# Three rounded passes for the inverse DFT-64 of seven batches, with new places for constants and weight loads

## The chip, the cores and the metric

The kernel runs on one core of a Trainium2 chip. The metric is the time of one execution on the device in microseconds (us), the median of several runs; less is better.

## What is computed

A Fourier mixing layer is followed by a gated feed-forward layer. Input x has 8 batches of 3008 rows and 256 columns; the model is 256 wide, the feed-forward layer 2048.

```python
X = np.fft.rfft(x, axis=1)
Xr, Xi = (X.real.astype(np.float32), X.imag.astype(np.float32))
Yr = Xr @ w_r - Xi @ w_i + b_r
Yi = Xr @ w_i + Xi @ w_r + b_i
Yr = np.sign(Yr) * np.maximum(np.abs(Yr) - lam, 0.0)   # lam = 0.01, Yi alike
y = np.fft.irfft(Yr + 1j * Yi, n=x.shape[1], axis=1)
h = y.reshape(B * S, D) @ w_in
g = h * (1.0 / (1.0 + np.exp(-1.702 * h)))
return (g @ w_out).astype(np.float32)
```

## The kernel before

**The Fourier part.** 3008 is 64 x 47, so the transform is done as a DFT of 47 and one of 64. For each batch, `spectral` lists the work in two halves. The first has 16 steps: `load_x` brings a piece of x, `stage_a` multiplies it by the DFT-47 constants on TensorE, ScalarE copies the result out (aev) and it is stored to a DRAM scratch. The second has 12 steps (sp), each for two frequencies of the DFT-47: `load_b` reads br back with its constants kr, `stage_b` does the forward DFT-64, `stage_mix` the product with w_r and w_i, the bias and the soft threshold (into mv), `move` carries mv by four DMAs into yr with real and imaginary rows stacked, and `stage_inv` does the inverse DFT-64 of yr, copies it out (iev) and stores it. `tokens` then reads it as ur, does the inverse DFT-47 and writes the columns of y that the feed-forward part reads. Stages lag each other: inverse step n - 5 stands beside forward step n.

**The feed-forward part.** It goes over 24 tiles of rows, and for each over 8 pieces q of the 2048 columns. From tile 2 on (PLAIN = 2) a product of 2x2 blocks is done with 7 products in place of 8. Weights arrive as float64 and are turned into pairs of rounded float32 numbers (`fetch`, `turn`, `combine`); `keep` writes the results to DRAM, from where `load_up` (wq), `Group.load` (wd) and `load_wo` (wo) fetch them again.

**Two ways to multiply.** A plain float32 matmul is one instruction in the program and two records in the trace. The other way splits both operands into a rounded part and a rest (`split`: ScalarE casts, VectorE subtracts) and does three passes in the float32r type (`mm3`, lines 147 to 149). The inverse DFT-64 is plain float32 in every batch (line 434), and its constants kv differ from step to step, so each `move` also loads 128 KB of kv into one of two buffers (KV = 2).

**Order and buffers.** A list scheduler sets the order of each engine when the kernel is built; at run time every engine and every DMA queue takes its work in that order. The Fourier steps of batches 1 and 2 fill tiles 0 and 1; those of later batches are spread over the tiles before they are due. The tag w2 is a pool of 7 buffers that xr, aev, br, mv, mt, yr, iev and ur share; the tag g has 13 for raw weights, x pieces and gelu results; wd has 3. SP issues nearly all DMAs; POOL issues the aev stores of batches 1 to 7, the raw weight loads of the main loop and the writes of `keep`.

Of the kernel before, what the change touches and what calls it, by code (L numbers as in the profile page):

```python
# [21 lines left out]
LAM = 0.01  # L22
# [5 lines left out]
TILE = 2 * TOK  # L28
NQ = DFF // 256
NP = 7  # L30
W2 = 7
PLAIN = 2
EARLY = 3
TK, JIT, RAW, WQ, WD, PT, KV, CO, ZT = 7, 3, 13, 3, 3, 5, 2, 1, 1
TINY = float(np.uint32(896 << 20).view(np.float32))


# [15 lines left out]
def constants():  # L53
    def ang(a, b, n):
        return 2.0 * np.pi * ((np.outer(a, b)) % n) / n

    n1, n2, k1, k2 = np.arange(N1), np.arange(N2), np.arange(N1), np.arange(NS)
    t47 = ang(n2, k2, N2)
    t64 = ang(n1, k1, N1)


    fa = np.zeros((48, NS, 2))
    fa[:N2, :, 0] = np.cos(t47)
    fa[:N2, :, 1] = -np.sin(t47)
# [24 lines left out]
    binv0 = inv * np.concatenate([w0r, w0i])[:, None]  # L89
    binv0[:, N1:] = 0.0  # L90


    ai = np.zeros((NS, 2, 2, 2, N2))
    for p in range(2):
        ai[:, 0, p, p] = np.cos(t47.T)
        ai[:, 1, p, p] = -np.sin(t47.T)
    ai = ai.reshape(96, 94)

    signs = np.ones((NS, 2 * N1, 1))
    signs[:, N1:, 0] = sign.T  # L100
    v = signs * binv
    v[0] = binv0
    v = v.reshape(NS // 2, 2, 2 * N1, 2 * N1).transpose(0, 2, 1, 3)
    kbs = np.stack([b, v], axis=1)

    pack = np.zeros((128, 190), np.float32)
    pack[:96, 0:96] = a
    pack[:96, 96:190] = ai
    return pack, kbs.astype(np.float32)


@with_exitstack
def fourier_mix_then_gated_ffn(ctx: ExitStack, tc: tile.TileContext, x, w_r, w_i, b_r, b_i, w_in, w_out, pack, kbs, out):
# [38 lines left out]
    kc = cst.tile([96, 192], F32, name="kc")[:, 0:190]  # L152
    nc.sync.dma_start(kc[:, 0:96], pack[:96, 0:96])
    ka32, kz = kc[:, 0:96], kc[:, 96:190]
    nlam = cst.tile([128, 16], F32, name="nlam")[:, 0:1]
    nc.vector.memset(nlam, -LAM)
    nc.scalar.activation(cst.tile([128, 16], F32, name="gelu_table")[:, 0:1], nlam, AF.Gelu_apprx_sigmoid)
# [6 lines left out]
    def later_constants():  # L164
        imag.append(buf([128, 2, D], F32, "wi", tag="co", bufs=CO))
        w3 = slot4([128, 2, 2, D], F32, "w3")
        wf32.extend((w3[:, 0], w3[:, 1], slot4([128, 2, D], F32, "wr")))
        for t, w in ((wf32[2], w_r), (imag[0], w_i)):
            with tc.issue_after(stored[9]):
                nc.sync.dma_start(t, w.rearrange("(c p) e -> p c e", p=128))  # L170

    def in_row(sp):
        last = later[-1]
# [12 lines left out]
            nc.vector.scalar_tensor_tensor(wf32[v], wf32[2], -1.0, imag[0], ALU.mult, op)  # L186

    def split_constants():
        for v in range(3):
            split(wf_h[:, v], wf_l[:, v], wf32[v])  # L190

# [1 line left out]
    kept = [dw.tile([128, 2 * NP * 128], F32, name=f"kept{q}") for q in range(NQ)]  # L193
    kept_o = [dw.tile([128, 4 * 256], F32, name=f"kept_o{q}") for q in range(NQ)]
    kept_d = [dw.tile([128, NP, 2, NQ // 2, 128], F32, name=f"kept_d{h}") for h in range(2)]
    up_w, wo, fresh = {}, {}, []

    raws = {}

# [46 lines left out]
    def turn(kind, q):  # L246
# [7 lines left out]
        nc.scalar.copy(w[:, 0], a)  # L254
        nc.vector.tensor_tensor(d, a, w[:, 0].bitcast(F32), ALU.subtract)
        nc.vector.tensor_tensor(w[:, 1], e, d, ALU.add)
        fresh.append((2, q, w))

    def combine(kind, q, a, e, wq):
        a, e = (t.rearrange("p c (f n) -> p c f n", f=2) for t in (a, e))  # L260
# [43 lines left out]
    def spectral(b, s2):  # L304
# [1 line left out]
        s1w = s1.rearrange("c p j d -> (c p) (j d)")  # L306
        s1r = s1.rearrange("(s r) p j d -> s (r p j) d", r=2)
        s2w = s2.rearrange("(s r) p j d -> s (r p j) d", r=2)
        xs, raw, zs, ys, ks, moves, mine = {}, {}, {}, {}, {}, {}, []

        plain, plain_a = b == 0, b < 3
        shared = []
# [8 lines left out]
            xs[2 * i], xs[2 * i + 1] = t[:, 0:2], t[:, 2:4]  # L321

        def load_x(q):
            xs[q] = slot4([128, 2, D], F32, "xa") if plain_a else buf2("xr")
            nc.sync.dma_start(xs[q][:96].rearrange("p j d -> p (j d)"), x[b, :, 512 * q:512 * (q + 1)])

        def split_x(q):
            if plain:
# [32 lines left out]
        def load_b(sp):  # L361
# [5 lines left out]
            if sp == 0:  # L367
                later.append(mine[13 if plain else 15])
            with tc.issue_after(later[-1]):
                nc.sync.dma_start(k, kbs[sp, 0])  # L370
# [27 lines left out]
        def stage_mix(sp):  # L398
# [12 lines left out]
            nc.vector.tensor_tensor(v, pb.rearrange("p (r e) -> p r e", r=2), v, ALU.add)  # L411

            nc.scalar.activation(t, v, AF.Relu, bias=nlam)
            last = nc.vector.scalar_tensor_tensor(v, v, LAM, t, ALU.add, ALU.min)
            if plain:
                mixed[:] = (last.ins,)

# [2 lines left out]

        def move(sp):
            y, v = moves.pop(sp)
            kv = ks[sp] = buf([128, 2, 2 * N1], F32, "kv", bufs=KV)
            nc.sync.dma_start(kv, kbs[sp, 1])
            for i in range(2):
                for r in range(2):
                    (nc.scalar if plain and sp == 11 and r == 1 else nc.sync).dma_start(y[64 * r:64 * r + 64, i], v[64 * i:64 * i + 64, r])

        def stage_inv(sp):
            y = ys.pop(sp)  # L430
            pv = bank().rearrange("p (s d) -> p s d", s=2)
            kv = ks.pop(sp)
            for i in range(2):
                done_inv.append(nc.tensor.matmul(pv[:, i], lhsT=kv[:, i], rhs=y[:, i], start=True, stop=True).ins)  # L434
            ev = buf2("iev")
            nc.scalar.copy(ev, pv)  # L436
            nc.sync.dma_start(s2w[2 * sp:2 * sp + 2].rearrange("s p d -> p s d"), ev)
# [6 lines left out]
            first += listed((0, split_x, n, 16), (650, stage_a, n, 16))  # L444
        late = 5 if plain else 5
        for n in range(12 + late):
            second += listed((900, stage_b, n, 12), (2000, stage_mix, n - 1, 12), (0, move, n - 1 if plain else n - 2, 12), (650, stage_inv, n - late, 12))
        def preload():
            for n in range(4):
                load_x(n)  # L450
# [179 lines left out]
    class Group:  # L630
# [197 lines left out]
    for n in range(NT * NQ):  # L828
# [25 lines left out]
        for i, p in enumerate(PATTERN + (0,) * (k < PLAIN)):  # L854
# [6 lines left out]
            else:  # L861
                for _ in range(2 if k + 1 == NT and q >= 4 else 1):
                    down()
            if i == 0 and n + EARLY < NQ:
                fetch(0, EARLY + n)
            if i == 4 and n + EARLY < NQ:
                with tc.issue_after(gelu[-1]):
                    turn(0, EARLY + n)
            if i == 5 and n + WQ < NQ:
                fetch(1, WQ + n)  # L870
            if i == 9 and n + WQ < NQ:
                with tc.issue_after(gelu[-1]):
                    turn(1, WQ + n)
# [1 line left out]
            if i == 9 and q2 is not None:  # L875
                with tc.issue_after(gelu[-1]):
                    combine(0, q2, wo[q2][:, 0].bitcast(F32), wo[q2][:, 1].bitcast(F32), None)
            if i % 5 == 2:
                fill(2)
                if i in (2, 12):  # L880
# [66 lines left out]
```

## Time and profile before

| What | Value |
|---|---|
| Median of the runs (lowest, highest) | 2533.74 us (2532.31, 2543.44) |
| The profiled execution, its span | 2537.07 us, 2534.9 us |
| TensorE busy (matmul) | 2472.7 us, 98% of the span |
| VectorE busy | 2032.7 us, 80% |
| ScalarE busy | 1872.5 us, 74% |
| DMA moved, mean rate | 558.46 MB, 220 GB/s |
| Share of TensorE in the chain that ended last | 89% |

Busy is the time in which an engine had an instruction running; matmuls overlap in the pipeline, so what one costs TensorE is read from start to start. Idle time of another engine counts only where TensorE waits for it in the end. In the timelines a bracket behind a row gives the idle time of that engine before it and what ended it.

### The profile page before, as it was taken

How to read it: one execution, taken by the hardware profiler on the slowest of the kernel's cores; microseconds unless marked ns; L12 is line 12 of the kernel's file. 1: busy time of each engine (PE TensorE's matmuls, PEld its weight loads, DVE VectorE, ACT ScalarE, POOL GpSimd, SP SyncE). 2: the span in 40 equal slices, each digit the busy share in tenths (PEclk: the TensorE clock that was granted, in tenths of full speed). 3: DMA queues.
4: the chain of work that ended last, by engine and by line, in shares of the span. 5: the costliest groups of instructions: out<-in, count | busy, mean ns of one | idle time of the engine just before them, and what ended most of it. 6: DMA issues, size and time to landing. Idle time of an engine off the chain costs nothing.

```text
span 2534.9 us, 35670 instructions
## 1 busy us (share of the span) xinstructions
PE 2472.7 (98%) x12270; PEld 2056.0 (81%) x12270; DVE 2032.7 (80%) x2587; ACT 1872.5 (74%) x3009; POOL 90.6 (4%) x160
## 2 busy tenths in 40 slices
PE   8789999999999999999999999999999999999998
PEld 5557878888688887888878887788878888888888
DVE  4668747988679887888878887889968988888984
ACT  4567657877778777777777777877777877877774
POOL 0121100000100001000010000000000000000000
PEclk9989999999999999999999999999999999999999
DMA  8767665666776677666776768657686666665563
GB/s 244 245 234 252 215 194 183 206 223 220 239 239 194 224 232 258 208 222 194 259 243 200 227 198 282 226 192 233 202 287 225 201 220 217 215 217 191 198 220 130
DMA packets 240226, 558.46 MB, mean 220 GB/s; under 512 B 28752, under 2 KB 129360, under 8 KB 240048
## 3 DMA queue, kind: packets, MB, share of 16 engines
q1 hardware_dynamic: 226640, 508.87, 61.7%
q0 software_dynamic: 13248, 47.20, 5.3%
q8 instruction: 99, 1.62, 0.3%
q14 instruction: 79, 0.65, 0.1%
q10 hardware_dynamic: 160, 0.13, 0.0%
HBM read 437.07 MB, written 93.85 MB: 209 GB/s over the span
## 4 chain that ended last, share of the span: by engine, by line
PE 89%; DMA 5%; DVE 3%; ACT 2%; issue 1%; SPq 0%; POOL 0%; ACTq 0%; DVEq 0%; POOLq 0%
PE pa L147 12%; PE pa L148 12%; PE pa L149 12%; PE po L147 11%; PE po L148 11%; PE po L149 11%; PE pa L475 4%; PE pa L342 4%; PE pa L388 3%; PE pa L434 3%; PE seed L147 2%; PE seed L149 2%; PE seed L148 2%; PE pa L405 1%; DMA s<-iev 1%
## 5 line engine op out<-in xcount | busy, mean ns | idle before, releaser
L144 DVE TENSOR_TENSOR gl<-g,gl 128x1024 fp32r<-128x1024 f32 (+3 forms) x672 | 763.3, 1145 | 187.9 <-ACT gl L144 186.2
L144 ACT CAST gl<-g 128x1024 fp32r<-128x1024 f32 (+3 forms) x672 | 659.9, 992 | 163.2 <-PE po L149 142.4
L147 PE MATMUL pa<-tk,wq 128*128 128x512 f32 (+1 forms) x1169 | 492.6, 422 | 9.4 <-ACT s L572 3.9
L147 PE MATMUL po<-gl,wd 128*128 128x512 f32 (+1 forms) x1176 | 466.3, 402 | 3.8 <-DVE pt L535 3.4
L148 PE MATMUL po<-gl,wd 128*128 128x512 f32 (+1 forms) x1176 | 464.3, 395 | 0.0
L149 PE MATMUL po<-gl,wd 128*128 128x512 f32 (+1 forms) x1176 | 458.7, 390 | 0.0
L148 PE MATMUL pa<-tk,wq 128*128 128x512 f32 (+1 forms) x1169 | 454.5, 389 | 0.1
L149 PE MATMUL pa<-tk,wq 128*128 128x512 f32 (+1 forms) x1169 | 451.7, 388 | 0.0
L659 DVE TENSOR_TENSOR g<-g 128x1024 f32<-128x1024 f32 (+1 forms) x336 | 402.1, 1206 | 12.2 <-ACT g L579 10.8
L578 DVE TENSOR_TENSOR g<-pa,s 128x512 f32<-128x512 f32 (+1 forms) x401 | 268.9, 675 | 85.9 <-PE pa L149 57.4
L572 ACT COPY s<-pa 128x512 f32<-128x512 f32 (+1 forms) x401 | 230.9, 577 | 97.8 <-PE pa L149 92.7
L579 ACT ACTIVATE g<-g 128x512 f32<-128x512 f32 (+1 forms) x401 | 249.2, 624 | 44.8 <-DVE g L578 43.9
L147 PEld LDWEIGHTS pa<-tk,wq 128*128 128x128 f32 x1169 | 221.5, 189 | 64.5 <-ACT s L572 8.5
L147 PEld LDWEIGHTS po<-gl,wd 128*128 128x128 f32 x1176 | 221.7, 189 | 52.7 <-DVE pt L535 5.0
L148 PEld LDWEIGHTS po<-gl,wd 128*128 128x128 f32 x1176 | 222.2, 189 | 46.4 <-issue 4.3
L149 PEld LDWEIGHTS po<-gl,wd 128*128 128x128 f32 x1176 | 221.8, 189 | 45.7 <-issue 2.5
L149 PEld LDWEIGHTS pa<-tk,wq 128*128 128x128 f32 x1169 | 220.3, 188 | 44.7 <-issue 0.4
L148 PEld LDWEIGHTS pa<-tk,wq 128*128 128x128 f32 x1169 | 221.5, 190 | 43.0 <-issue 10.6
L535 DVE TENSOR_TENSOR pt<-po,pt 128x512 f32<-128x512 f32 (+1 forms) x210 | 142.5, 678 | 18.6 <-PE po L149 18.2
L475 PEld LDWEIGHTS pa<-kc,ur 96*128 96x128 f32 x1024 | 137.1, 192 | 18.3 <-issue 4.4
L147 PE MATMUL pa<-wf_h,zt 128*128 128x256 f32 x504 | 142.8, 283 | 0.2 <-ACT iev L436 0.2
L149 PE MATMUL pa<-wf_h,zt 128*128 128x256 f32 x504 | 142.3, 282 | 0.0
(119 smaller groups left out, 3444.2 us busy)
## 6 DMA issues: line engine op xcount, KB each, us to landing
wq<-kept SPq DMA_DIRECT2D x184, 896.0 KB, 5.2
wd<-kept_d SPq DMA_DIRECT2D x294, 512.0 KB, 3.9
br<-s SPq DMA_DIRECT2D x96, 256.0 KB, 4.1
s<-iev SPq DMA_DIRECT2D x96, 256.0 KB, 3.4
ur<-s SPq DMA_DIRECT2D x128, 192.0 KB, 4.4
yr<-mv SPq DMA_DIRECT2D x382, 64.0 KB, 2.9
out<-pt SPq DMA_DIRECT2D x88, 256.0 KB, 4.2
s<-aev POOLq DMA_DIRECT2D x112, 192.0 KB, 4.0
```

The costliest lines, as they stand in the source:

```text
L144: return nc.scalar.copy(hi, src).ins, nc.vector.tensor_tensor(lo, src, hi.bitcast(F32), ALU.subtract).ins
L147: nc.tensor.matmul(ps, lhsT=wh, rhs=xh, start=start, stop=False, skip_group_check=more)
L148: nc.tensor.matmul(ps, lhsT=wh, rhs=xl, start=False, stop=False, skip_group_check=more)
L149: nc.tensor.matmul(ps, lhsT=wl, rhs=xh, start=False, stop=stop, skip_group_check=more)
L342: ins = nc.tensor.matmul(ps[:96], lhsT=ka32, rhs=xs.pop(q), start=True, stop=True).ins
L388: nc.tensor.matmul(pv[:, c, :, i], lhsT=t[:, i, cs], rhs=k[:, i], start=True, stop=True)
L475: turned.append(nc.tensor.matmul(pv[:, c, 94 * j:94 * j + 94], lhsT=t[:, j, 128 * c:128 * c + 128], rhs=kz, start=True, stop=True).ins)
L535: nc.vector.tensor_tensor(t, ps[:, :w], t, ALU.add)
L572: nc.scalar.copy(t, ps[:, :self.w])
L578: nc.vector.tensor_tensor(t, ps[:, :w], self.s[other], ALU.add)
L579: gelu[:] = (nc.scalar.activation(t, ps[:, :w] if other is None else t, AF.Gelu_apprx_sigmoid).ins,)
L659: nc.vector.tensor_tensor(out, x, y, ALU.subtract)
```

## The change

1. **The inverse in three passes.** In batches 1 to 7 the new step `split_y` splits yr into yh and yl (two w2 buffers), and `stage_inv` calls `mm3`: one group of three passes 512 columns wide, or for step 0, whose two halves have different constants, two groups 256 wide. Batch 0 keeps plain float32.
2. **One set of inverse constants.** The sign that made kv differ from step to step is multiplied into the imaginary half of mv instead (a 128x256 multiplication on ScalarE, with a column of the new constant fk, in all batches). ki then holds all inverse constants; it is loaded once and split once into kir. All loads of kv go.
3. **Loads of x.** For batches 1 and 2 one DMA brings two pieces.
4. **Feed-forward weights.** Raw loads are asked for earlier in the program, the write-back of w_out's pieces later, and the first two pieces of w_out are asked for within the last group before the last tile.
5. **Buffers.** w2 has 8 in place of 7; the two of kv go.

```diff
-W2 = 7
+W2 = 8
@@ constants
-    kbs = np.stack([b, v], axis=1)
+    pack[:, 192:320] = binv
+    pack[:, 320:448] = binv0
+    pack[:, 448:460] = sign.T.reshape(NS // 2, 2 * N1).T
+    return pack, b.astype(np.float32)
@@ later_constants
+        with tc.issue_after(stored[9]):
+            nc.sync.dma_start(fk, pack[:, 448:464])
+            nc.sync.dma_start(ki.rearrange("p v n -> p (v n)"), pack[:, 192:448])
@@ split_constants
+        split(kir[:, 0], kir[:, 1], ki)
@@ turn
-        fresh.append((2, q, w))
+        spare.append((2, q, w))
@@ load_x
+            if plain_a and q % 2 == 0:
+                t = slot4([128, 4, D], F32, "xa")
+                nc.sync.dma_start(t[:96].rearrange("p j d -> p (j d)"), x[b, :, 512 * q:512 * (q + 2)])
+                xs[q], xs[q + 1] = t[:, 0:2], t[:, 2:4]
@@ stage_mix
-            last = nc.vector.scalar_tensor_tensor(v, v, LAM, t, ALU.add, ALU.min)
+            nc.vector.scalar_tensor_tensor(v, v, LAM, t, ALU.add, ALU.min)
+            last = nc.scalar.mul(v[:, 1], v[:, 1], fk[:, sp:sp + 1])
             if plain:
                 mixed[:] = (last.ins,)
@@ move
-            kv = ks[sp] = buf([128, 2, 2 * N1], F32, "kv", bufs=KV)
-            nc.sync.dma_start(kv, kbs[sp, 1])
@@ new
+        def split_y(sp):
+            if not plain:
+                yh, yl = (buf([128, 2, D], F32R, n, tag="w2", bufs=W2) for n in ("yh", "yl"))
+                split(yh, yl, ys[sp])
+                ys[sp] = yh, yl
@@ stage_inv
-                done_inv.append(nc.tensor.matmul(pv[:, i], lhsT=kv[:, i], rhs=y[:, i], start=True, stop=True).ins)
+            elif sp == 0:
+                for i in range(2):
+                    mm3(pv[:, i], kir[:, 0, 1 - i], kir[:, 1, 1 - i], y[0][:, i], y[1][:, i])
+            else:
+                mm3(pv, kir[:, 0, 0], kir[:, 1, 0], *y)
@@ the list of the second half
+(0, split_y, n - late + 1, 12),
@@ Group.load
+            elif self.tile.k + 2 == NT and self.q0 + self.n == NQ:
+                load_wo(at - len(self.PHASES))
@@ main loop
+    fetch(0, EARLY)
+    fetch(1, WQ)
-            if i == 0 and n + EARLY < NQ:
-                fetch(0, EARLY + n)
+            if i == 7 and n + 1 + EARLY < NQ:
+                fetch(0, 1 + EARLY + n)
-            if i == 5 and n + WQ < NQ:
-                fetch(1, WQ + n)
+            if i == 11 and n + 1 + WQ < NQ:
+                fetch(1, 1 + WQ + n)
+            if i == 6 and n > 5 and spare:
+                fresh.append(spare.pop(0))
```

Three places show what the scheduler makes of it. Lines of the changed kernel are a little higher: its `split` is line 140, `stage_mix` 418 to 423, `move` 434, the copy of iev 454.

**ScalarE at the end of batch 0.** First the order before, from the threshold of step 10 (mt0_704) on; mv_730 and yr0_736 belong to the last step, 11.

```order
L413 ACTIVATE mt0_704<-mv_703,nlam_76 128x512
L436 COPY iev_719<-pa_716 128x512
L230 ACTIVATE wae_745<-wraw_743 128x512
L436 COPY iev_762<-pa_759 128x512
L413 ACTIVATE mt0_731<-mv_730,nlam_76 128x512
L234 ACTIVATE wm_746<-wraw_743 128x512
L254 CAST wo_754<-wae_745 128x512
L436 COPY iev_768<-pa_765 128x512
L427 DMA yr0_736<-mv_730 64x256 x2
L436 COPY iev_774<-pa_771 128x512
```

The same in the changed kernel, where mv_736 and yr0_743 belong to step 11:

```order
L421 ACTIVATE mt0_737<-mv_736,nlam_79 128x512
L454 COPY iev_751<-pa_748 128x512
L454 COPY iev_757<-pa_754 128x512
L423 ACTIVATE mv_736<-mv_736,fk_78 128x256
L140 CAST kir_77<-ki_76 128x256
L140 CAST wf_h_84<-w3_207 128x512 x2
L140 CAST wf_h_84<-wr_208 128x512
L454 COPY iev_763<-pa_760 128x512
L434 DMA yr0_743<-mv_736 64x256 x2
```

Between the last threshold and the two moves that ScalarE issues there now stand the multiplication, the cast of kir and three casts of wf_h; the conversions of raw weights have moved away from there.

**POOL in tile 0.** The order before; s<-aev are batch 1's stores, wraw raw weights, kept and kept_o the write-back of w_in's and w_out's pieces.

```order
L358 DMA s_105<-aev 96x512
L283 DMA kept_83<-wq 128x1792
L285 DMA kept_o_91<-wo 128x1024
L285 DMA kept_o_92<-wo 128x1024
L358 DMA s_105<-aev 96x512 x3
L285 DMA kept_o_93<-wo 128x1024
L215 DMA wraw<-in_w_in 128x2x256
L358 DMA s_105<-aev 96x512
L285 DMA kept_o_94<-wo 128x1024
L358 DMA s_105<-aev 96x512
L215 DMA wraw<-in_w_out 128x2x256
L358 DMA s_105<-aev 96x512
```

The same stretch of the changed kernel:

```order
L218 DMA wraw<-in_w_out 128x2x256
L218 DMA wraw<-in_w_in 128x2x256
L366 DMA s_108<-aev 96x512
L286 DMA kept_86<-wq 128x1792
L366 DMA s_108<-aev 96x512 x3
L218 DMA wraw<-in_w_out 128x2x256
L366 DMA s_108<-aev 96x512
L218 DMA wraw<-in_w_in 128x2x256
L366 DMA s_108<-aev 96x512 x2
L286 DMA kept_87<-wq 128x1792
```

A raw load of w_in that stood behind the stores of a stretch now stands before them (the next one behind 11 stores in place of 14), and no kept_o is left here: all eight stand together further down, behind batch 1's last store.

**ScalarE at the end of batch 1.** The order before, from the threshold of the last step on; gl0 are the casts that feed the second product of the feed-forward part.

```order
L413 ACTIVATE mt_3112<-mv_3111,nlam_76 128x512
L579 ACTIVATE g0_3148<-g0_3148 128x512
L144 CAST gl0_3151<-g0_3148 128x512
L436 COPY iev_3163<-pa_3160 128x512
L572 COPY s_3142<-pa_3126 128x512
L436 COPY iev_3188<-pa_3185 128x512
L572 COPY s_3172<-pa_3126 128x512
L436 COPY iev_3197<-pa_3194 128x512
```

A little later in the changed kernel; yr_3006 and yr_3113 hold steps 10 and 11.

```order
L454 COPY iev_3190<-pa_3186 128x512
L140 CAST gl0_3147<-g0_3173 128x512
L140 CAST yh_3196<-yr_3006 128x512
L140 CAST gl0_3241<-g0_3239 128x512
L597 ACTIVATE g0_3253<-g0_3253 128x512
L454 COPY iev_3204<-pa_3200 128x512
L140 CAST yh_3207<-yr_3113 128x512
L140 CAST gl0_3241<-g0_3253 128x512
```

Casts of yr now stand between the casts of gl0. On SP, the four moves that fill yr_3113 stand shortly ahead of its cast. yh_3196 takes the w2 slot of iev_3162, whose store SP issues shortly before, and yh_3207 that of mv_3106, which the last moves read.

## Rows read from the trace of the kernel before

**Rows 1.** Busy time by stretch: PE, PEld, DVE, ACT, POOL; clock, DMA share, GB/s.

```profile
110.00:200.00 90.00, 76.61 (x248) 47.74 (x249) 59.94 (x115) 57.82 (x106) 25.56 (x44) 0.89 0.74 250
...
340.00:372.00 32.00, 27.43 (x131) 21.25 (x129) 10.28 (x16) 14.86 (x27) 1.77 (x2) 1.00 0.66 205
...
1000.00:2200.00 1200.00, 1198.08 (x6029) 1000.99 (x6028) 1015.96 (x1193) 926.55 (x1450) 25.17 (x49) 1.00 0.69 225
```

**Rows 2.** Timeline of TensorE around one inverse step: start, length, what.

```profile
1162.34 0.39 PE L147 MATMUL pa<-tk,wq 128*128 128x512 f32 x1
...
1163.02 1.02 PE L434 MATMUL pa<-yr,kv 128*128 128x256 f32 x4
...
1164.11 0.40 PE L147 MATMUL pa<-tk,wq 128*128 128x512 f32 x1
```

**Rows 3.** The same, passes 256 columns wide.

```profile
1028.00 0.28 PE L147 MATMUL pa<-wf_h,zt 128*128 128x256 f32 x1
...
1028.95 0.40 PE L147 MATMUL pa<-tk,wq 128*128 128x512 f32 x1
```

**Rows 4.** Groups by line and shape: total us, mean ns | idle before, releaser.

```profile
L147 PE MATMUL pa<-wf_h,zt 128*128 128x256 f32 x504 | 142.8, 283 | 0.2 <-ACT iev L436 0.2
...
L144 DVE TENSOR_TENSOR tk<-y,tk 128x512 fp32r<-128x512 f32 x154 | 103.3, 685 | 36.1 <-ACT tk L144 35.8
...
L144 ACT CAST tk<-y 128x512 fp32r<-128x512 f32 x154 | 92.9, 622 | 5.2 <-DVE y L517 2.7 <-PE pa L149 2.1
...
L500 ACT COPY y<-yx 128x248 f32<-128x248 f32 x1 | 0.4, 427 | 0.0
```

**Rows 5.** Busy time by stretch, as in Rows 1.

```profile
1100.00:1250.00 150.00, 149.51 (x774) 127.73 (x773) 131.44 (x155) 115.24 (x179) 0.00 (x0) 1.00 0.70 224
450.00:500.00 50.00, 50.00 (x250) 42.45 (x249) 48.07 (x61) 40.13 (x64) 0.00 (x0) 1.00 0.60 199
```

**Rows 6.** Waits by line, timelines of ScalarE and TensorE, and DMA landings.

```profile
DVE mv L410 <- DMA s<-iev: 10.4, 6, 4.8
...
351.45 0.72 ACT L413 ACTIVATE mt<-mv,nlam 128x512 f32<-128x512 f32 x1 [4.64 <-DMA s<-iev]
...
353.55 1.13 PE L434 MATMUL pa<-yr,kv 128*128 128x256 f32 x4 [1.71 <-DVE g L578]
...
s<-iev SPq DMA_DIRECT2D x96, 256.0 KB, 3.4
```

**Rows 7.** SP's own waits, and waits of TensorE: total us, times, longest.

```profile
SPq L424 <- PE pa L434: 110.9, 68, 6.8
...
PE pa L434 <- DMA kv<-in_kbs: 4.6, 4, 2.9
```

**Rows 8.** End of batch 0: TensorE, ScalarE's DMA issues, and their median landing.

```profile
95.69 1.10 PE L434 MATMUL pa<-yr,kv 128*128 128x256 f32 x4 [2.94 <-DMA kv<-in_kbs]
...
89.62 0.51 ACTq L427 DMA_DIRECT2D yr<-mv  x1
...
yr<-mv ACTq DMA_DIRECT2D x2, 64.0 KB, 2.4
```

**Rows 9.** Tile 0: timelines of ScalarE, TensorE and POOL; busy time by stretch.

```profile
154.24 0.66 ACT L230 ACTIVATE wae<-wraw 128x512 f32<-128x512 f32 x1 [2.91 <-DMA wraw<-in_w_in]
...
156.02 0.79 PE L147 MATMUL po<-gl,wo 128*128 128x512 f32 x1 [4.82 <-ACT gl L144]
...
134.51 0.54 POOL L358 DMA_DIRECT2D s<-aev  x1 [8.77 <-ACT aev L357]
...
147.37 0.73 POOL L215 DMA_DIRECT2D wraw<-in_w_in  x1
...
150.00:163.00 13.00, 8.18 (x24) 6.01 (x23) 7.72 (x18) 5.45 (x9) 0.74 (x1) 0.74 0.45 150
```

**Rows 10.** Busy time by stretch, as in Rows 1.

```profile
190.00:215.00 25.00, 23.15 (x98) 15.68 (x99) 20.36 (x40) 18.76 (x35) 7.36 (x13) 1.00 0.92 318
```

**Rows 11.** The chain that ended last, in order of time.

```profile
2474.12 6.84 DMA wo<-kept_o
```

More of the change, by code (lines that the diff above doesn't have):

```diff
@@ L30 @@
 NP = 7
-W2 = 7
+W2 = 8
 PLAIN = 2
 EARLY = 3
-TK, JIT, RAW, WQ, WD, PT, KV, CO, ZT = 7, 3, 13, 3, 3, 5, 2, 1, 1
+TK, JIT, RAW, WQ, WD, PT, CO, ZT = 7, 3, 13, 3, 3, 5, 1, 1
 TINY = float(np.uint32(896 << 20).view(np.float32))
@@ L97, in constants @@
     ai = ai.reshape(96, 94)
[L99 to L103, printed above, removed]
-    kbs = np.stack([b, v], axis=1)
-    pack = np.zeros((128, 190), np.float32)
+    pack = np.zeros((128, 464), np.float32)
     pack[:96, 0:96] = a
     pack[:96, 96:190] = ai
-    return pack, kbs.astype(np.float32)
+    pack[:, 192:320] = binv
+    pack[:, 320:448] = binv0
+    pack[:, 448:460] = sign.T.reshape(NS // 2, 2 * N1).T
+    return pack, b.astype(np.float32)
 @with_exitstack
@@ L154, in fourier_mix_then_gated_ffn @@
     ka32, kz = kc[:, 0:96], kc[:, 96:190]
+    ki = cst.tile([128, 2, 128], F32, name="ki")
+    kir = cst.tile([128, 2, 2, 128], F32R, name="kir")
+    fk = cst.tile([128, 16], F32, name="fk")
     nlam = cst.tile([128, 16], F32, name="nlam")[:, 0:1]
@@ L195, in fourier_mix_then_gated_ffn @@
     kept_d = [dw.tile([128, NP, 2, NQ // 2, 128], F32, name=f"kept_d{h}") for h in range(2)]
-    up_w, wo, fresh = {}, {}, []
+    up_w, wo, fresh, spare = {}, {}, [], []
     raws = {}
@@ L308, in spectral @@
         s2w = s2.rearrange("(s r) p j d -> s (r p j) d", r=2)
-        xs, raw, zs, ys, ks, moves, mine = {}, {}, {}, {}, {}, {}, []
+        xs, raw, zs, ys, moves, mine = {}, {}, {}, {}, {}, []
         plain, plain_a = b == 0, b < 3
@@ L323, in load_x @@
         def load_x(q):
-            xs[q] = slot4([128, 2, D], F32, "xa") if plain_a else buf2("xr")
-            nc.sync.dma_start(xs[q][:96].rearrange("p j d -> p (j d)"), x[b, :, 512 * q:512 * (q + 1)])
+            if plain_a and q % 2 == 0:
+                t = slot4([128, 4, D], F32, "xa")
+                nc.sync.dma_start(t[:96].rearrange("p j d -> p (j d)"), x[b, :, 512 * q:512 * (q + 2)])
+                xs[q], xs[q + 1] = t[:, 0:2], t[:, 2:4]
+            elif not plain_a:
+                xs[q] = buf2("xr")
+                nc.sync.dma_start(xs[q][:96].rearrange("p j d -> p (j d)"), x[b, :, 512 * q:512 * (q + 1)])
         def split_x(q):
@@ L369, in load_b @@
             with tc.issue_after(later[-1]):
[L370 removed]
+                nc.sync.dma_start(k, kbs[sp])
             later.append(nc.sync.dma_start(t, s1r[2 * sp:2 * sp + 2].rearrange("s p d -> p s d")).ins)
@@ L431, in stage_inv @@
             pv = bank().rearrange("p (s d) -> p s d", s=2)
-            kv = ks.pop(sp)
-            for i in range(2):
-                done_inv.append(nc.tensor.matmul(pv[:, i], lhsT=kv[:, i], rhs=y[:, i], start=True, stop=True).ins)
+            if plain:
+                for i in range(2):
+                    done_inv.append(nc.tensor.matmul(pv[:, i], lhsT=ki[:, int(sp == i == 0)], rhs=y[:, i], start=True, stop=True).ins)
+            elif sp == 0:
+                for i in range(2):
+                    mm3(pv[:, i], kir[:, 0, 1 - i], kir[:, 1, 1 - i], y[0][:, i], y[1][:, i])
+            else:
+                mm3(pv, kir[:, 0, 0], kir[:, 1, 0], *y)
             ev = buf2("iev")
@@ L446, in spectral @@
         for n in range(12 + late):
-            second += listed((900, stage_b, n, 12), (2000, stage_mix, n - 1, 12), (0, move, n - 1 if plain else n - 2, 12), (650, stage_inv, n - late, 12))
+            second += listed((900, stage_b, n, 12), (2000, stage_mix, n - 1, 12), (0, move, n - 1 if plain else n - 2, 12), (0, split_y, n - late + 1, 12), (650, stage_inv, n - late, 12))
         def preload():
```

## The prediction, made before the changed kernel ran

> **What bounds the kernel now.** I read the busy time by stretch first [rows 1]. From 1000 to 2200 us TensorE is busy 1198.1 of 1200 us while VectorE has 1016.0 and ScalarE 926.6: there the time is the number of matmul passes times their spacing. Time that is not matmul lies elsewhere: 13.4 us of idle TensorE from 110 to 200 us, with a granted clock of 0.89, and 4.6 us from 340 to 372. So I went to the matmul rows for what a pass costs, to the costs of the new ScalarE and VectorE work, and then to the three places where TensorE sat idle and the change moves something: the end of batch 0, tile 0, and the end of batch 1.
>
> **The matmuls of the inverse.** One step (two 128x256 float32 products, four records in the trace) starts at 1163.02; the second pass after it starts at 1164.11 [rows 2]. Take off one ordinary pass of 0.227 (three of them lie between 1162.34 and 1163.02) and a step costs 1.09 - 0.227 = 0.863 us. Three rounded passes 512 columns wide cost 3 x 0.227 = 0.681. Step 0 of each batch has two different constants and so six passes 256 wide; eight such passes take 0.95 us [rows 3], six take 0.71. With 12 steps in each of 7 batches: 77 x 0.182 + 7 x 0.15 = **-15.1 us**. It counts in full where TensorE is the bound and not at all where something else is; batch 0 keeps its float32 products.
>
> **What ScalarE and VectorE get.** 84 casts of 128x512 at 0.622 us (52 us), 84 subtractions at 0.685 (58 us) and 96 multiplications of 128x256 on ScalarE, priced by a 128x248 copy out of SBUF at 0.427 (41 us) [rows 4]. If all of it lay on the path the kernel would lose 151 us; if none, nothing. The nearest row is the split of zt: the same pair of casts and subtractions feeds the mix matmuls, 84 times, and TensorE waited 0.2 us in all before those 504 passes [rows 4]. For the middle of a batch I therefore take the hidden end. VectorE has room, not much: 131.4 of 150 us in the second half of a batch (1100 to 1250), where 12 subtractions add 8.2 us, which makes 139.6 of about 148. From 450 to 500 it was busy 48.1 of 50 and TensorE still all 50 [rows 5].
>
> **The shared w2 buffers.** A step took five of seven (br, mv, mt, yr, iev); now it takes seven of eight, since yh and yl are added. A writer waits until its slot's last user is done, often a DMA: VectorE waited 10.4 us in 6 places for a store of iev to land before it could write mv [rows 6]. Both queues are in order, so everything behind waits too. In the order of the changed kernel such waits for a landing get closer together. At the end of batch 1 the casts of the last two steps stand behind a store or a move issued shortly before them, with TensorE's gl casts behind them. Bounds: 0, if all is covered as in the middle; or, at each of the 7 batch ends, one store's and one move's landing in line, 3.4 + 2.4 = 5.8 us [rows 6, 8], which is 41 us. The second needs every end to be bare of other matmuls; from 1000 to 2200, where four batches end, TensorE was idle 1.9 us altogether [rows 1]. Nearer to zero, then: **+5 us**, about what the end of batch 1 alone cost from 340 to 372.
> The first of those waits is there to see. At 351.45 ScalarE had stood 4.64 us for a landing, and TensorE idled at 353.55 for 1.71 us behind it [rows 6]. The Trainium skill's page "Perfetto Trace Analysis", section "Tensor Engine Instruction (MATMUL, LD_WEIGHTS)", says that ScalarE and VectorE take their work strictly in order; by that rule a cast that waits for a move holds back gelu and every split behind it, and the time would be that of rival D. The trace agrees with the rule at that place.
>
> **kv is no longer loaded.** 96 loads of 128 KB go. SP stood 110.9 us for their slots [rows 7], mostly beside other work; TensorE waited 4.6 us for kv over the run [rows 7], 2.94 of it in batch 0 [rows 8]. The rest is **-1.7 us** (between 0 and -4.6).
>
> **End of batch 0.** The last product waited those 2.94 us, until 95.69. What is next late there? The moves of the last step. Two of them are issued by ScalarE, at 89.62 before. Now they stand behind the new multiplication, the cast of kir and three casts of wf_h, which hang on the last mix instruction, and this one is now ScalarE's: 2 x 0.43 + 3 x 0.62 = 2.7 us [rows 4], so about 92.3 and 92.9, and landed 2.4 us later [rows 8] at 95.3, against 95.69 before. The wait gets a new name: **0** (-1 to +2). The loads of xa, now in pairs, stand at the same place behind the loads of ur: 0.
>
> **Tile 0.** ScalarE waited 2.91 us until 154.24 for the weights of w_in, TensorE idled 4.82 us until 156.02 behind it, and the stretch 150 to 163 had a granted clock of 0.74 [rows 9]. That load left the POOL queue at 147.37 because it stands behind fourteen stores of aev. In the changed order it stands behind eleven; the eleventh store left at 134.51 [rows 9], so the load lands some 12 us sooner and the 2.91 us go. The clock fell to the 1.2 GHz level after the idle stretch: 26% of 13 us is 3.4 us lost. An idle stretch of 1.9 us may or may not cause that; I take half. **-4.6 us** (0, if the next wait takes its place; -13 if the idle time of 110 to 200 mostly goes). The load of w_out before it keeps its six stores ahead, so its wait stays.
> The writes of w_out's pieces (eight of 512 KB) now leave POOL in one burst right after batch 1's last aev store; before they stood between those stores. In 190 to 215, while the last of the stores go out, the DMA share was already 0.92, and TensorE was busy 23.15 of 25 us [rows 10]. I take **+1** (0 to +2, as much again as the idle time of that stretch). The Trainium skill's "DMA: Bandwidth & Descriptors", section "Issuing engines are not separate DMA queues", says that POOL's and SP's transfers run on the same 16 engines and interleave; by that the burst takes time from SP's loads and the term belongs at +2, and without it at 0. No row before shows such a burst.
>
> **The end.** TensorE waited there for the first piece of w_out, loaded at 2474.12 in 6.84 us [rows 11]. The change asks for it in an earlier place of the program, but on SP it stands between the same neighbours as before, since it needs a slot of wd; the last 80 instructions of SP and the last 761 of TensorE are unchanged. **0**.
>
> **The sum** is -15.1 + 5 - 1.7 + 0 - 4.6 + 1 + 0 = -15.4 us. The profiled execution took 2537.07 us (span 2534.9 and 2.2 around it), 3.3 above the median of 2533.74; the sum gives 2521.7 for it and 2518 for the median.
>
> **The rivals.** A difference of 0.5%, 12.7 us (2521.1 and 2546.4), is about what a measurement can tell from no change.
> A, the forecast, 2518: chance 0.40, of which 0.30 lies under 2521.
> B, tile 0 gives back more: the idle time and the low clock of 110 to 200 feed each other, so one wait less may free the next. With -13 there and the w2 term at 0: -15.1 - 1.7 - 13 = -30, or 2504. For it: the clock of 0.89 over 90 us. Against it: only one of the waits there has its cause moved. 0.20.
> C, VectorE takes over the second half of the batches: at 139.6 of 148 us plus waits for slots it has no slack, TensorE's 15.1 us turn into waits for gl and zt, and the rest of the sum without the w2 term, -5.3, stays: 2528. For it: the 88% of VectorE now. Against it: the 48.1 of 50. 0.20.
> E, the change doesn't do in tile 0 what its code says: the loads leave POOL when the slots come free and not earlier, the wait moves on. -15.4 + 4.6 = -10.8: 2523. 0.10.
> D, slower: the casts of the last steps put ScalarE in line for a store and a move at every batch end, as at 351.45. Price 5.8 us at each of 7 ends, +41, against -20.4 for the rest without the w2 term: +20, 2554. From 2.9 us per end the gain is eaten; from 4.7 the kernel is slower by more than 0.5%. For it: the order at those ends. Against it: at ends other than the first TensorE had other matmuls to run. 0.10.
>
> **How the numbers follow.** Faster by over 0.5%: 0.30 of A and B, 0.50. Within: 0.10 of A, C and E, 0.40. Slower: 0.10. The range goes from B's 2504 less 2 to the forecast with half of the upper w2 bound in place of its 5 (2518 - 5 + 20.5 = 2534) and without tile 0's 4.6: 2538. It leaves out D and the far side of B.
>
> **What would show it.** Right: passes yh,kir at 0.227 from start to start, TensorE's records from 1000 to 2200 closed up; no ScalarE wait for w_in near 154; the idle time before the last product of batch 0 still there, now released by yr. Wrong: waits of ScalarE or VectorE on yr, s or mv before yh and yl with idle TensorE behind them (C, D), or idle time at 2474 gone (then the early load of w_out does something after all).

## The result, and the profile after

The changed kernel takes 2550.85 us (median; 2547.80 to 2554.54), against 2535.39 for the kernel before, run beside it: a ratio of 1.0056, 95% interval 1.0043 to 1.0068. It is slower by some 14 us. Forecast were 2518 us and a range that ends at 2538, so both the sign and the range are wrong. The profiled execution has a span of 2547.1 us, 12.2 more than before.

Busy time by stretch of the changed kernel (PE, PEld, DVE, ACT, POOL; granted clock, DMA share, GB/s), the rows that answer to [rows 1] and [rows 5]:

```profile
110.00:200.00 90.00, 79.25 (x286) 50.51 (x286) 64.84 (x126) 62.06 (x115) 23.19 (x40) 0.94 0.75 242
...
340.00:372.00 32.00, 27.95 (x128) 21.75 (x126) 12.02 (x20) 17.52 (x33) 0.90 (x1) 0.96 0.68 214
...
1000.00:2200.00 1200.00, 1182.17 (x5898) 978.20 (x5896) 1024.41 (x1219) 946.55 (x1517) 24.57 (x48) 0.99 0.68 217
...
1100.00:1250.00 150.00, 149.10 (x765) 125.77 (x764) 134.86 (x162) 121.02 (x197) 0.00 (x0) 1.00 0.67 214
```

Look at the third row. From 1000 to 2200 us TensorE was idle 1.9 us before; now it is idle 17.8 us, in the stretch where the forecast wanted its records closed up. VectorE is not full there. So something makes all engines wait.

To see how much, I gave each matmul record the start-to-start spacing that its shape has at full clock when passes follow each other (0.227 us for 512 columns in three-pass products, 0.428 for float32) and called "excess" what is left of the time from the first matmul to the last:

| us | sum of spacings | excess | of it to 110 | 110 to 205 | 205 to 2190 | from 2190 |
|---|---|---|---|---|---|---|
| before | 2421.3 | 104 | 25 | 25 | 33 | 22 |
| changed | 2406.2 | 132 | 26 | 20 | 68 | 18 |
| e2_plain (below) | 2421.3 | 88 | 24 | 20 | 19 | 24 |
| e9_raw12_w10 (below) | 2406.2 | 96 | 26 | 19 | 37 | 14 |

Tile 0 gave back 5 us; the middle of the run lost 34. The 15.1 us between the sums of spacings are counted, not measured: they follow from the number of records and the fixed spacings. In the trace the three passes stand 0.23 us from start to start, a little more than the forecast 0.227:

```profile
1158.31 0.40 PE L143 MATMUL pa<-yh,kir 128*128 128x512 f32 x1
1158.54 0.39 PE L144 MATMUL pa<-yl,kir 128*128 128x512 f32 x1
1158.77 0.40 PE L145 MATMUL pa<-yh,kir 128*128 128x512 f32 x1
1159.01 0.39 PE L143 MATMUL pa<-tk,wq 128*128 128x512 f32 x1
```

That is 0.70 us for a step (the median of the undisturbed steps is 0.702) in place of the forecast 0.681, and 0.707 for step 0. Against 0.863 before, the products give back 77 x 0.161 + 7 x 0.156, some 13.5 us; the other 1.6 us are part of the excess.

Who waits in the middle? These are waits for transfers between 650 and 2150 us in the changed kernel (engine and line, what it waited for: us in all, times, longest):

```profile
ACT iev L454 <- DMA yr<-mv: 11.4, 8, 2.6
DVE mv L418 <- DMA s<-iev: 9.3, 4, 4.6
DVE yl L140 <- DMA yr<-mv: 6.2, 3, 4.2
PE pa L350 <- DMA xr<-in_x: 9.4, 5, 2.9
PEld pa L350 <- DMA xr<-in_x: 8.3, 4, 3.3
```

and in the kernel before, with its own line numbers:

```profile
ACT iev L436 <- DMA yr<-mv: 6.2, 5, 1.9
DVE mv L410 <- DMA s<-iev: 5.5, 5, 1.9
PE pa L342 <- DMA xr<-in_x: 3.7, 3, 2.6
```

The first two rows are the key to the kind of wait. The copy into iev does not read yr or mv, and the addition into mv does not read iev. Such a wait is for a w2 buffer: in all 8 waits of the first row the buffer that iev is given had been mv's, and is not free until the moves out of it have landed; in all 4 of the second mv takes over a buffer of iev. The third row is of the same kind: yl reads yr, but yr had landed 8 us or more before; the buffer that yl is given was mv's. Summed over all such rows of that stretch, ScalarE, VectorE and TensorE waited 19.8, 15.5 and 11.6 us for transfers (before: 11.6, 8.6 and 4.7).

One place in mid batch shows how such a wait reaches TensorE. ScalarE's timeline (start, length; in brackets idle time before and what ended it):

```profile
1213.15 0.59 ACT L590 COPY s<-pa 128x512 f32<-128x512 f32 x1
1216.36 0.59 ACT L454 COPY iev<-pa 128x512 f32<-128x512 f32 x1 [2.63 <-DMA yr<-mv]
1216.84 1.05 ACT L140 CAST gl<-g 128x1024 fp32r<-128x1024 f32 x1
1217.79 0.60 ACT L597 ACTIVATE g<-pa 128x512 f32<-128x512 f32 x1
```

and TensorE's behind it:

```profile
1218.44 0.50 PE L143 MATMUL pa<-tk,wq 128*128 128x512 f32 x1 [0.48 <-ACT g L597]
```

ScalarE takes its work in order. While the copy waits, the gelu behind it waits, and with it the bank that the next matmul needs. Here 2.63 us cost TensorE half a microsecond. From 650 to 2200 us the gaps over 1 us between matmuls make 13 us of the loss (none were there before), 10 of them before products that read xr; the rest comes in such small pieces and in matmuls at a lower clock (below).

At a batch start the gap of TensorE is larger. SP's and TensorE's timelines:

```profile
1549.41 0.89 SPq L333 DMA_DIRECT2D xr<-in_x  x2
...
1550.86 0.84 SPq L333 DMA_DIRECT2D xr<-in_x  x1
...
1556.34 1.42 PE L350 MATMUL pa<-xr,kc 96*96 96x512 f32 x2 [2.40 <-DMA xr<-in_x]
```

Before, the first load of this batch left earlier, into a buffer that was iev's:

```profile
1546.83 0.97 SPq L325 DMA_DIRECT2D xr<-in_x  x1
```

By the order of the program the first three of these loads take over the buffers of the yl and yh of the last inverse steps. But the products that read those end between 1546.6 and 1548.0, and each load left some 3 us after its buffer was free. So none of the three waits for w2. They stand late in SP's order, behind a store of iev and loads of wq and ur, and the first was 6.9 us on its way (5.9 before). Whether the shortage makes them late, by way of that order, is not shown here. The wait itself cost twice (stretches in the columns of above):

```profile
1553.00:1557.00 4.00, 1.60 (x8) 0.84 (x6) 4.00 (x5) 2.92 (x5) 0.00 (x0) 1.00 1.04 318
1557.00:1560.00 3.00, 3.00 (x7) 1.60 (x6) 2.99 (x3) 0.58 (x1) 0.51 (x1) 0.50 0.84 241
```

After the wait TensorE runs at a granted clock of 0.50, its 1.2 GHz level, until 1560. With a second such stretch, 1868 to 1876 (last section), 11 us ran at half the full clock; by an estimate from these rows that is up to 5.5 of the 34 us.

### The profile page after: what moved, and what is told of

It reads as the page before. It is cut to its first block, busy times and chain, and to the rows that moved or that the text cites. A ratio compares the mean times of both kernels' runs of the same rounds, so it can differ in the third digit from the quotient of the medians.

```text
span 2547.1 us, 35726 instructions
## 1 busy us (share of the span) xinstructions
PE 2474.5 (97%) x12207; PEld 2044.3 (80%) x12207; DVE 2080.4 (82%) x2672; ACT 1944.6 (76%) x3190; POOL 90.0 (4%) x160
## 4 chain that ended last, share of the span: by engine, by line
PE 82%; DMA 6%; DVE 5%; ACT 4%; issue 2%; SPq 1%; POOL 0%; ACTq 0%; DVEq 0%; POOLq 0%
PE pa L143 12%; PE pa L144 12%; PE pa L145 12%; PE po L143 10%; PE po L144 10%; PE po L145 10%; PE pa L493 4%; PE pa L350 4%; PE pa L396 3%; PE seed L143 2%; PE seed L144 2%; PE seed L145 2%; DMA xr<-in_x 1%; DVE gl L140 1%; DMA yr<-mv 1%
## 5 line engine op out<-in xcount | busy, mean ns | idle before, releaser
L143 PEld LDWEIGHTS pa<-tk,wq 128*128 128x128 f32 x1169 | 221.6, 190 | 78.6 <-ACT s L590 15.5
```

Source lines behind the costliest of these rows:

```text
L143: nc.tensor.matmul(ps, lhsT=wh, rhs=xh, start=start, stop=False, skip_group_check=more)
```

## The experiments

Ratios are to the kernel before, run on the same chip in the same round; 5 rounds each. Names of buffers and lines are those of the changed kernel. The list scheduler makes a new order for each version, so an expectation's "order" or "listing" that stays is that of the program's list of steps, not that of the engines.

**Taking the change apart.** Theory S: yh and yl, two more tenants of the eight w2 buffers, hold up all the others. Theory W: the cast and the subtraction themselves, in order on their engines, do the harm. Theory P: the rest of the change does.

e1_inplace, one buffer less in use per step:

```diff
-yh, yl = (buf([128, 2, D], F32R, n, tag="w2", bufs=W2) for n in ("yh", "yl"))
+yh, yl = buf([128, 2, D], F32R, "yh", tag="w2", bufs=W2), ys[sp].bitcast(F32R)
```

> The changed kernel, but yl is written over yr, so a step of the inverse takes one more w2 buffer and not two; work, order and products stay. Theory S (the two extra tenants of the eight w2 buffers hold up the loads of xr, the copies iev and the moves, and TensorE waits mid-run for these): most of the 35 us that TensorE's spacings show over the nominal work between 110 and 2200 us goes, 2525 to 2540 us. Theory W (the cast and the subtraction themselves, in order on ScalarE and VectorE, hold up what stands behind them): nothing moves, 2547 to 2555 us.

e2_plain, no split at all:

```diff
         def split_y(sp):
-            if not plain:
+            if False:
...
         def stage_inv(sp):
...
-            if plain:
+            if True:
```

> The changed kernel with the inverse in plain float32 in every batch (no cast, no subtraction, no yh, no yl); the fetch moved earlier, the merged loads of batches 1 and 2, the sign multiplied on ScalarE and eight w2 buffers stay. S and W alike: the products cost 15 us more and the mid-run waits go, 2524 to 2533 us, under the kernel before by the gains of tile 0 and of the end. Theory P (the sign multiplication on ScalarE in every batch or the moved fetches did the harm): 2555 to 2570 us.

e5_work, the work of the split without its buffers (the diff is shortened: the inverse is plain as in e2_plain, and the split of its constants goes too):

```diff
-yh, yl = (buf([128, 2, D], F32R, n, tag="w2", bufs=W2) for n in ("yh", "yl"))
-split(yh, yl, ys[sp])
-ys[sp] = yh, yl
+yd = buf([128, 2, D], F32R, "yd", bufs=1)
+split(yd, yd, ys[sp])
...
```

> As e2_plain, but the cast and the subtraction of each step of batches 1 to 7 are carried out, at the same places, into one buffer of their own that no product reads; the products read yr in plain float32 and no w2 buffer is held by yh or yl. Theory W: 20 to 35 us over e2_plain. Theory S: within 6 us of e2_plain.

e3_before_w8, the kernel before:

```diff
-W2 = 7
+W2 = 8
```

> The kernel before with eight w2 buffers in place of seven. Theory S holds the more strongly the more a buffer is worth here: 2522 to 2531 us. If buffers were not short with seven: within 3 us of the kernel before, and then S needs that yh and yl take more than the eighth buffer gives.

| | median us | ratio | 95% interval |
|---|---|---|---|
| changed kernel | 2550.9 | 1.0056 | 1.0043 to 1.0068 |
| e1_inplace | 2537.2 | 1.0000 | 0.9986 to 1.0015 |
| e2_plain | 2522.4 | 0.9931 | 0.9913 to 0.9948 |
| e5_work | 2534.5 | 0.9982 | 0.9969 to 0.9995 |
| e3_before_w8 | 2539.9 | 0.9999 | 0.9986 to 1.0012 |

P falls: all but the three passes is a gain of 0.7%. The three passes with their split cost 1.0056 - 0.9931 = 1.25% of 2535, 32 us, of which one buffer (e1) takes back 14 with the work unchanged: S. e5 lies 13 us over e2, between what S and what W expected. It is not a clean price of the work, since the list scheduler put its casts right behind the moves: by the trace they start a median of 3.6 us after the last of the four moves is issued, and ScalarE stood for the landings (in the changed kernel the distance is 33.7 us, and as much in e9 below with ten buffers):

```profile
ACT yd L140 <- DMA yr<-mv: 62.9, 43, 2.9
```

In the kernel before the eighth buffer is worth nothing.

**Giving buffers.** How long is a buffer held? From its first write to its last use, by trace and program order, between 650 and 2150 us: in the kernel before mv 26 us and yr 43 us; in the changed one mv 25, yr 37, yh 13, yl 11. Together that is 5.4 of 7 buffers in use on average before, 6.0 of 8 after, landings not counted. By this average the changed kernel has more room to spare than the kernel before, 2.0 buffers against 1.6; it does not tell that one is short and the other is not.

e9_raw12_w10 has two more buffers:

```diff
-W2 = 8
+W2 = 10
-TK, JIT, RAW, WQ, WD, PT, CO, ZT = 7, 3, 13, 3, 3, 5, 1, 1
+TK, JIT, RAW, WQ, WD, PT, CO, ZT = 7, 3, 12, 3, 3, 5, 1, 1
```

> The changed kernel with ten w2 buffers and not eight, the room taken from the raw buffers (twelve and not thirteen); products, work and listing stay. Theory S: the two buffers that yh and yl need are there, 2512 to 2530 us, less what the raw buffer cost (0 to 8 us). Theory W: 2547 to 2558 us.

f4_w9 has W2 = 9 and f3_raw12_only W2 = 8, both with RAW = 12.

> e9 with nine w2 buffers. Theory S, with e1_inplace as the size of one buffer (14 of the 38 us): 2525 to 2540 us, between the changed kernel and e9. If the order is merely shaken: anywhere, outside that range.

> Control of e9: the changed kernel with twelve raw buffers and still eight w2 buffers. Theory S: no gain, 2547 to 2560 us. If the smaller raw pool itself (another placement of everything behind it) gave e9 its time: under 2535 us.

c1_before_raw12_w10 is the kernel before with the same two numbers (10 and 12), c2_plain_raw12_w10 is e2_plain with them.

> Control of e9: the kernel before with ten w2 buffers and twelve raw buffers. If e9's 1.5% over the changed kernel came from buffers that yh and yl need: within 0.3% of the kernel before, 2531 to 2546 us. If ten buffers speed up any version of this kernel: 2510 to 2528 us.

> e2_plain with ten w2 buffers and twelve raw buffers: e9 without the three passes. If the three passes are a gain once the buffers are there: 2518 to 2528 us, like e2_plain, and e9 (0.9905) lies under it by the 15 us of the products less what the cast and the subtraction cost. If not: 2505 to 2515 us.

| w2 buffers (12 raw buffers) | changed kernel | plain inverse (e2) | kernel before |
|---|---|---|---|
| 8 | 1.0060 (f3: 1.0042 to 1.0078) | | |
| 9 | 0.9972 (f4: 0.9956 to 0.9987) | | |
| 10 | 0.9905 (e9: 0.9891 to 0.9918) | 0.9921 (c2: 0.9903 to 0.9938) | 0.9981 (c1: 0.9969 to 0.9994) |

This settles S. The smaller raw pool gains nothing (f3); each buffer gives the changed kernel 0.7 to 0.9%, 39 us for two; the same change gives the plain kernel 0.1% (c2 against e2; c2's 2517.4 us lies between its two ranges) and the kernel before 0.2%. The shortage is that of yh and yl. One rival has to be named: with other buffers the scheduler also orders the work anew. Against f3, some three in ten of ScalarE's instructions stand in another order in e9. A new order alone has brought nothing like 39 us: against the kernel before it is two in ten in e3 and one in four in c1, with ratios of 0.9999 and 0.9981. How much of the 39 us comes from waits that go and how much from a better order that more buffers allow is not shown. In e9's trace the rows of above are smaller, and from 1000 to 2200 TensorE is idle 9.1 us in place of 17.8:

```profile
ACT iev L454 <- DMA yr<-mv: 3.7, 3, 2.6
DVE yl L140 <- DMA wd<-kept_d: 4.6, 1, 4.6
DVE yl L140 <- DMA yr<-mv: 1.5, 1, 1.5
PE pa L350 <- DMA xr<-in_x: 4.6, 4, 2.5
1000.00:2200.00 1200.00, 1190.89 (x5984) 990.60 (x5983) 1042.47 (x1243) 965.83 (x1549) 24.57 (x48) 1.00 0.68 219
```

No row of VectorE waiting for iev's store to free mv's buffer is left; the wait of 4.6 us that names wd ends as the moves out of mv land, whose buffer that yl takes. Summed as above, the three engines waited 8.0, 6.5 and 5.8 us. These sums do not measure the loss, though. With nine buffers (f4) the kernel is 0.9% faster than with eight, yet ScalarE's sum is 22.8 us, more than the 19.8 of the changed kernel; what has shrunk is TensorE's waits for xr:

```profile
ACT iev L454 <- DMA yr<-mv: 15.4, 8, 3.1
PE pa L350 <- DMA xr<-in_x: 1.4, 1, 1.4
```

What the three passes bring once they have room is e9 against c2: 0.16%, 4 us, less than the two intervals tell apart; of the 13.5 us some 9.5 are taken by something else.

**Holding buffers for a shorter time.** e6_late4 and e7_late4_inplace:

```diff
-late = 5 if plain else 5
+late = 5 if plain else 4
```

> The changed kernel with the inverse of a step of batches 1 to 7 listed four steps behind its stage_b and not five (the split goes with it, and so stands one step behind the move and not two); products, work and buffers stay. In the changed kernel's trace a yr buffer is held 37 us and yh, yl 13 and 11 us, some 2.4 of the eight buffers together; a step is some 15 us, so this gives back about 0.6 of a buffer. Theory S (buffers): 2532 to 2546 us. Theory W (the cast and the subtraction wait in order for the landing of the move): the distance to the move shrinks, 2552 to 2570 us.

> e6_late4 with yl written over yr, as in e1_inplace. Theory S: the two gains add up as long as buffers are still short, 2518 to 2532 us. Theory W: 2538 us (e1_inplace) or more.

e6 is 1.0061 (1.0048 to 1.0074), 2553.7 us: no gain, in W's range and not in S's. yr is held 22 us in place of 37, but yh and yl 15 and 13 in place of 13 and 11, and the casts now wait longer for moves to land, 16.4 us in the run in place of 3.7:

```profile
ACT yh L140 <- DMA yr<-mv: 16.4, 8, 3.5
```

About half of these 16.4 us, 4 waits at the ends of batches, are for the cast's own yr; the others are for a buffer of mv. In the changed kernel all of the 3.7 us are for buffers: no cast there waits for its own yr. e7 is 0.9939 (0.9927 to 0.9951), 0.6% under e1, as S expected. With ten buffers the same step hurts (w3 below). So it is no clean measure of the shortage; a step moved earlier gives room and takes lead away.

**Which tenant is hurt.** f1_xa takes the loads of x out of w2 (and brings them in pairs, asked for three pieces ahead and not two):

```diff
-plain, plain_a = b == 0, b < 3
+plain, plain_a = b == 0, b < 8
```

> The changed kernel with the loads of x of batches 3 to 7 in the 4096-byte buffers that batches 1 and 2 use for them (512 KB-class pairs in place of single loads), out of the eight w2 buffers; the rest as changed. If the loads of x at the batch starts are the main victim of the shortage: 2515 to 2530 us. If it is the copies, casts and moves in mid batch: 2535 to 2550 us.

It is 1.0061 (1.0043 to 1.0078), 2555.1 us, outside both ranges, and told nothing apart: TensorE waited as long for the loads in their new pool:

```profile
PE pa L350 <- DMA xa<-in_x: 10.8, 6, 3.4
```

It is no clean test, as a pair takes a median of 7.1 us to land and a single load 4.8. But it agrees with 1549.41 above: the loads came late although they took no w2 buffer, and SP stood under 4 us at them from 650 to 2150, against 35 in the changed kernel. How the 34 us are shared between batch starts and mid batch is thus known only by the size of the gaps, as above.

**What else the change gained.** c3_plain_old_rest undoes in e2_plain the earlier fetches, the paired loads of x, the later use of w_out's spare tiles and the early wo load:

```diff
-            if i == 7 and n + 1 + EARLY < NQ:
-                fetch(0, 1 + EARLY + n)
+            if i == 0 and n + EARLY < NQ:
+                fetch(0, EARLY + n)
...
```

> e2_plain with the fetches, the merged loads of batches 1 and 2, the split of w_out's spare tiles and the load of wo where the kernel before has them; what stays of the change is the inverse from constants (no kv loads), the sign on ScalarE and eight w2 buffers. Theory F (the moved fetches and loads gave e2_plain its 0.7%): 2531 to 2540 us. Theory K (the kv loads that are gone, with all that SP has to issue behind them, gave it): 2518 to 2527 us.

e8_before_kv5 gives the kernel before more room for kv:

```diff
-TK, JIT, RAW, WQ, WD, PT, KV, CO, ZT = 7, 3, 13, 3, 3, 5, 2, 1, 1
+TK, JIT, RAW, WQ, WD, PT, KV, CO, ZT = 7, 3, 13, 3, 3, 5, 5, 1, 1
```

> The kernel before with five kv buffers and not two; nothing else. The trace of before has SP waiting 110.9 us in all at the kv load for an inverse product to free one of two buffers, with the moves of yr and the loads of xr and wd queued behind it. Theory K (this is what the plain kernel of the first round of experiments gained, 12 of its 17 us of excess between 205 and 650 us): 2524 to 2531 us. If the loads were free, as the prediction had it: within 3 us of the kernel before.

c3 is 0.9959 (0.9944 to 0.9975). So the moved fetches and loads are worth 0.3%, 7 us, and what is left, the missing kv loads with the sign on ScalarE and an eighth buffer, 0.4%, 10 us. The eighth buffer alone gave nothing (e3). e8 is 0.9992 (0.9978 to 1.0006), no gain, but it does not take away what it was meant to: SP still waits at the kv load, 71.8 us in place of 110.9 [rows 7]:

```profile
SPq L424 <- PE pa L434: 71.8, 41, 6.1
```

Why the missing loads bring 10 us, by SP's wait or by their transfers, stays open.

**Versions that beat both.** w1_w10_inplace is e9 with yl over yr; w3_w10_inplace_late4 has late = 4 on top.

> e9 (ten w2 and twelve raw buffers) with yl written over yr. If buffers are still short with ten: 2504 to 2511 us. If ten are enough: 2511 to 2518 us.

> w1 (ten buffers, yl over yr) with the inverse four steps behind its stage_b, as in e7. If the yr buffers still count: 2503 to 2510 us. If ten are enough: within 4 us of w1 (2512 us).

w1 is the fastest version, 2512.2 us, 0.9895 (0.9878 to 0.9913), though not told apart from e9: ten are about enough. w3 is 0.9959 (0.9938 to 0.9979): its expectation, gain or no change, was wrong by 0.6%. Its casts stand close behind their moves, and nearly all of ScalarE's waits at them are for their own yr, at the ends of batches; that this is the whole 0.6% is not shown. In w1, ScalarE waits for landings of moves between 650 and 2150 us

```profile
ACT yh L140 <- DMA yr<-mv: 1.3, 2, 0.7
ACT iev L454 <- DMA yr<-mv: 0.5, 1, 0.5
```

and in w3

```profile
ACT yh L140 <- DMA yr<-mv: 6.6, 4, 2.9
ACT yh L140 <- DMA s<-iev: 3.1, 1, 3.1
```


## Why the prediction was wrong, step by step

**The w2 buffers: the step that failed.** The prediction counted that a step now takes seven of eight buffers in place of five of seven, gave the bounds 0 and 41 us, and took 5, "nearer to zero", because TensorE was idle only 1.9 us from 1000 to 2200 [rows 1]. f3 against e9 measures 39 us. The choice within the bounds failed. That the upper bound of 41 lies so near is luck: it was made of casts that stand in line for landings at 7 batch ends, and what the rows show is copies, additions and subtractions that wait for buffers in mid batch (1216.36). The row that the choice rested on shows that five tenants fit into seven buffers and says nothing on seven in eight. Average held times would not have told either: 5.4 of 7 was enough, 6.0 of 8 was not. The long waits of TensorE at batch starts (1556.34), where the forecast had not looked at all, are shorter in all where buffers are given (9.4 us, 4.6 in e9); by what path is open.

**Rival D** comes nearest to what happened: ScalarE and VectorE do stand in line for stores and moves. Its number, 2554 us forecast and 2551 measured, is luck. Its casts hardly waited (3.7 us over the run, for buffers), and the price of 5.8 us at each of 7 ends is not in the rows. It was given 0.10. "At ends other than the first TensorE had other matmuls to run" was the argument against it; in mid batch it had, but their gelu stood behind the waiting copy. The rule of the Trainium skill's page "Perfetto Trace Analysis", section "Tensor Engine Instruction (MATMUL, LD_WEIGHTS)", on strict order that the prediction set beside D is borne out by the rows at 1216.36.

**The matmuls**, -15.1: nearly right. The passes follow each other at 0.234 and not 0.227, which makes some -13.5.

**ScalarE and VectorE**, priced at 0: not quite. With ten buffers some 9.5 us of the 13.5 are missing (e9 against c2, within intervals of some 5 us), and e5 shows 13 for work that stands close behind its move. What takes them is not shown. Rival C did not come: VectorE has 134.9 of 150 us, forecast 139.6.

**kv**, -1.7 with -4.6 as the end: too small. c3 and e3 give about -10 for the missing loads together with the sign on ScalarE, beyond the bound, which was made from TensorE's own waits for kv alone.

**End of batch 0**, 0 (-1 to +2): the moves on ScalarE leave at 96.07 and 96.64, not at 92.3, and the last product starts 2.5 us later than in [rows 8], just beyond the end of the range:

```profile
95.53 0.52 ACT L423 ACTIVATE mv<-mv,fk 128x256 f32<-128x256 f32 x1
95.94 0.40 ACT L140 CAST kir<-ki 128x256 fp32r<-128x256 f32 x1
96.07 0.53 ACTq L434 DMA_DIRECT2D yr<-mv  x1
...
98.20 1.40 PE L447 MATMUL pa<-yr,ki 128*128 128x256 f32 x4 [1.61 <-DVE wf_l L140]
```

The bracket names the split of the constants, but in the program this product waits for the moves of yr and, of VectorE, only for a step of mv that ended at 93.86; the move of 96.07 landed at 98.06. So it is yr that is late, as forecast, though not for the reason given: the move left as the multiplication ended (96.05) and did not stand behind the casts. Late was the last threshold, at 93.95 in place of 88.14.

**Tile 0**, -4.6 and +1 for the burst: right in sum. Excess from 110 to 205 falls by 5, and e2 against c3 gives 7 for all moved fetches and loads, with intervals of some 4 us. The wait of [rows 9] for w_in is gone, another took its place (3.72 us before 159.16, for a product of VectorE), and the clock there did not fall; the burst of writes shows no cost, the DMA share of 190 to 215 is 0.78, against 0.92 in [rows 10]:

```profile
159.16 0.94 ACT L140 CAST wq<-w 128x896 fp32r<-128x896 f32 x1 [3.72 <-DVE w L273]
...
150.00:163.00 13.00, 11.35 (x43) 7.46 (x42) 8.43 (x18) 7.95 (x14) 2.21 (x4) 1.00 0.65 201
190.00:215.00 25.00, 23.78 (x110) 17.30 (x109) 20.59 (x45) 19.06 (x35) 8.17 (x15) 1.00 0.78 283
```

**The end**, 0: the chain still ends in the wait for wo, as in [rows 11]:

```profile
2490.22 5.67 DMA wo<-kept_o
```

With what the runs measured in place of the forecast terms the sum is -13.5 (products) + 37 (the shortage: 39, less the 2.5 us that the same two buffers give the plain kernel) + 9.5 (what else the split costs) - 10 (kv and sign) - 7 (fetches and loads), +16 us; measured are +14. That it comes out is no proof of the terms: they are differences between runs on the way from the kernel before to f3 (1.0060), so they add up to f3's 15 us.

## What to carry to other kernels

Before you add a tile to a shared pool, do not trust that the pool is wide enough because it was; neither the count of tenants nor the average number in use told it here. Run the kernel with one and two buffers more, and give the same buffers to the kernel before, as f3, f4, e9 and c1 do. When an engine waits for a transfer whose data it does not read, ask what last used the buffer that it writes; such a wait stops all that is queued behind it on that engine. Cheaper products can cost more than they give while the operands' new buffers lack room: here the same passes cost 32 us with eight buffers, and with ten they cost nothing.

## What the runs showed of the hardware

A wait of TensorE in mid run can cost more than its length. After the 2.40 us before 1556.34 the granted clock was 0.50 from 1557 to 1560, and after a wait of 2.89 us that ended at 1867.95 it was 0.50 up to 1876, though TensorE was busy all of it; in the kernel before the stretch from 1000 to 2200 has a clock of 1.00. It does not always come so: in e9 TensorE waited 2.53 us before 1533.54, and the clock stayed at 1.00 (last row).

```profile
1868.00:1872.00 4.00, 4.00 (x7) 2.01 (x8) 2.91 (x3) 0.58 (x1) 0.51 (x1) 0.50 0.61 199
1872.00:1876.00 4.00, 4.00 (x14) 3.20 (x13) 0.00 (x0) 1.05 (x2) 0.51 (x1) 0.50 0.32 99
...
1533.00:1537.00 4.00, 3.46 (x14) 2.53 (x15) 1.91 (x2) 1.09 (x2) 0.51 (x1) 1.00 0.79 263
```

A transfer that ScalarE issues need not wait for the work listed before it on that engine: the move above left at 96.07, while the cast of kir listed before it ran until 96.34.
